# Loading and turning keys by pairs of heads, and VectorE alone for the first outer products, in a linear-attention and two-MoE kernel

## The chip, the core and the metric

One of the eight cores of a Trainium2 chip runs the program. Times are device microseconds (us) of one launch: the median of 3 runs of the kernel before is 305.4 (305.36, 305.4 and 305.83). Engines: PE is TensorE (PEld its weight loads), DVE VectorE, ACT ScalarE, POOL GpSimd, SP SyncE, which here only issues DMAs (SPq in the profile is its queue).

## The reference, cut to what matters

```python
def phi(x):                                   # x: batch 4, heads 4, seq 1088, dim 32; S1, S2: 8 x 32
    a = einsum('rd,bhsd->bhsr', S1, x)
    b = einsum('rd,bhsd->bhsr', S2, x)
    return outer product of a and b per token  # 64 features
q_p, k_p = phi(q), phi(k)
kv  = einsum('bhsf,bhsd->bhfd', k_p, v)
z   = sum of k_p over the sequence
x   = (q_p @ kv) / (q_p @ z + 1e-6)           # 4352 tokens x 128
xn  = x / rms(x) * rms_g                      # first MoE: 128 -> 1536 -> 128
x   = (silu(xn @ w_gate) * (xn @ w_val)) @ w_out
# second (soft) MoE: logits = x @ phi; softmax over tokens and over 32 slots; 8 experts of width 1024
```

S1, S2 and the weights of the first MoE come as 64-bit floats and are converted on the chip.

## The kernel before, in words

The 4352 tokens are nine tiles T: tiles 0 to 7 have 512 tokens each (tile T belongs to batch T // 2), tile 8 holds the last 64 tokens of every batch and head. For every tile the first MoE runs in twelve slots f of 128 hidden columns: `ff_in` makes the gate and value products g and v (lines 695 to 697, three matmuls each, since xh/xl and wgh/wgl are a high and a low part of the numbers), `ff_gate` the silu and the product hh or hf (lines 736, 737), `ff_out` the product with w_out. Queries of later tiles (`q_chain`) and keys of later batches (`k_chain`) are prepared between the slots.

Before the first slot stands the **front**: keys of batch 0 and queries of tile 0, since `ff_in` of tile 0 needs them. Its order is written by hand in the table `FRONT`, a list of tokens; every token is a step, and `in_order` keeps each engine's instructions in the order of the tokens. Outside of the front and its LOCK of 3 slots a scheduler of the build decides. The steps that matter here, with lines of the kernel before:

- `load_k`, `load_v`, `load_q`, `load_kr`: DMAs, all issued by SP in the order of the calls (line 79). `kt` is the key tile, `kr` the last 64 keys of every head, `vt` the values, `q0s` the first half of the queries of batch 0.
- `kt:c` (line 367) transposes a half of the keys on DVE into a tile T, `kt:2` the small keys (line 370), `qs` the queries (line 545).
- `b` and `bm` make the projection tables: bdk (line 304), for the keys, and bd (line 306), for queries and small keys.
- `kp` projects the keys on PE (line 388), `kg` the small keys (line 392), `qp` the queries (line 550).
- `kx:hp` (line 396) turns the projections of a pair hp of heads on DVE, `kh` (line 314) and `qh` (lines 314 and 557) copy them out of PSUM on ACT.
- `ko:g` and `qo:f` (line 319) are the outer products: `ko:0` and `ko:1` for the two pairs of heads, `ko:2` for the small keys, `qo:0` and `qo:1` for the queries. The letter behind is the engine (d is DVE, p is POOL, which can't read PSUM: `qh` therefore copies both halves for it).
- `kv:hp` copies V beside a column of ones (line 375, ACT, tile va).
- `ks:hp` sums over the tokens on PE (line 427: sixteen matmuls on the large keys, then two on the small ones), `kw` spreads the sums (line 442, ACT), `kb` transposes them (line 452, PE), `kl` places them as kvz (line 469: four copies for each pair).
- `qb` (line 565) turns the outer products of the queries, `qa` is the product with kvz (line 582), and `qd`, `qq`, `qr`, `qm`, `qt`, `qx`, `ql` are division, norm and the two parts xh and xl.
- `n:17` issues 17 matmuls on constants (line 333), whose results nobody reads. `c:g` is one step of converting weight group g: on ACT lines 217 and 270, on DVE lines 221 and 226, on POOL lines 233 and 278.

Wherever two steps name the same engine, the table decides which stands first; an engine that waits for an operand holds up all that stands behind it.

Of the kernel before, what the change touches and what calls it, by code (L numbers as in the profile page):

```python
# [8 lines left out]
F32 = mybir.dt.float32  # L9
# [7 lines left out]
P = 128  # L17
B, H, S, D, R = 4, 4, 1088, 32, 8
# [12 lines left out]
FRONT = """  # L31
n:17 b n:3 kz kt:0 bm kt:1 bm qs kp kt:2 kx:0 kx:1 ko:0:d ko:1:p:0 ko:1:d:1 qp kg kv:0 kv:1 qh kh ko:2:d qo:1:p n:4 km
ks:0 qo:0:d qb c:0 ks:1 kw:0:a kb:0 kw:1:a n:2 kb:1 n:10 c:0 c:0 kl:0:a kl:1:d c:0 c:1 c:0 c:1 c:0 c:0
qa n:34 qd:0 qd:1 qq:0:a qq:1:d qr:0 qq:2:a qq:3:d qr:1 c:1 kr:a qm:0 qm:1 qt:0 qx:0 n:2 qt:1 qx:1 c:1 c:1 ql c:2 c:2 c:2 c:1 c:2
# [16 lines left out]
def body(ctx, tc, q, k, v, s1, s2, wg, wv, wo, rg, phi, w1, w2, out):  # L51
# [24 lines left out]
    gate = [None]  # L76

    def load(out, in_, on=None):
        i = (on or nc.sync).dma_start(out=out, in_=in_)
        if gate[0] is not None:  # L80
            info = mybir.DependencyInfo(mybir.DependencyClass.Sync, mybir.DependencyReason.DATA)
            tc.add_manual_dep(i.ins, gate[0], info, reason="load in time")
# [13 lines left out]
    def load_k(b):  # L96

        t = ring()
        kt[b] = t.rearrange("p (h c m) -> p h c m", h=H, c=2)
        src = k[b, :, 0:1024, :].rearrange("h (c u e n) d -> c e u h (n d)", c=2, e=2, n=4)  # L100
        for c in range(2):
            for e in range(2):
                load(out=kt[b][64 * e : 64 * e + 64, :, c], in_=src[c, e])

# [4 lines left out]
    def load_v(b):  # L109

        t = ring()
        vt[b] = t.rearrange("p (h n d) -> p h n d", h=H, d=D)
        load(
            out=t.rearrange("p (h n) -> p h n", h=H),
            in_=v[b, :, 0:1024, :].rearrange("h (p j) d -> p h (j d)", j=8),
        )
        load(out=vr[:, :, 0:D], in_=v[b, :, 1024:, :].rearrange("h p d -> p h d"))
# [36 lines left out]
    load_k(0)  # L154
    rest_q = load_q(0)
    load_kr(0)
    load_v(0)
    load_w(w_keys[0])
    rest_q()
# [191 lines left out]
    class Keys:  # L351
# [12 lines left out]
        def transpose(self, c):  # L364
            if c < 2:
                self.kT[c] = row("T", 2)
                dve.transpose(self.kT[c].rearrange("p (h m) -> p h m", h=H), kt[self.b][:, :, c])
            else:
                self.kT[c] = sb.tile([P, 64], F32, tag="krT", name="krT")
                dve.transpose(self.kT[c].rearrange("p (x n) -> p n x", n=2), kr[self.b])  # L370
# [5 lines left out]

        def project(self, banks=1):
            for h in range(H):
                if h == 0 or h == 2 and banks == 2:
                    a = bank()  # L380
                self.a["k", h // 2] = a
                cs = slice(P * h, P * h + P)
                for c in range(2) if banks == 2 else (1, 0):
                    with ExitStack() as s:
                        s.enter_context(tc.issue_after(self.last) if self.last else nullcontext())
                        o = a[64 * c : 64 * c + 64, cs]
                        s.enter_context(tc.high_priority())
                        self.last = pe.matmul(o, bdk.rearrange("p h r -> p (h r)"), self.kT[c][:, cs], start=True, stop=True).ins

# [73 lines left out]

        def place_1(self, f, eng):
            av = self.a["T", 2 * f].rearrange("p (m e n) -> p m e n", e=2, n=64)[:, :, :, 0:D1]
            hv = self.kvz.rearrange("p f (a e) g c -> p (f a) e g c", e=2)
            for g in range(4):
                gs = slice(32 * g, 32 * g + 32)
                eng(hv[gs, 2 * f : 2 * f + 2, :, g % 2, :], av[gs, 2 * f : 2 * f + 2])
# [60 lines left out]
    class Queries:  # L530
# [21 lines left out]
        def halves(self):  # L552
            self.pq = work()[:, 0 : 256 * self.n].rearrange("p (f g n) -> p f g n", f=2, n=D)
            self.x1, self.x2 = proj_halves(self.a["q"], 4 * self.n, P)
            if self.T == 0:
                x2 = sb.tile([P, P], F32, tag="asb", name="asb", bufs=3).rearrange("p (g r) -> p g r", r=R)
                act.copy(x2, self.x2)
                self.x2 = x2

# [100 lines left out]
    def q_chain(T):  # L660
        q = Queries(T)

        with tc.issue_after(mark["gate", 1, 0] if T == 2 else mark["sq0"]) if T < 3 else nullcontext():
            q.shuffle()
# [244 lines left out]
    def spawn(c, phase, at=0):  # L909
        chains.append([c, phase, now + at])  # L910
# [45 lines left out]
    def front():  # L956
# [13 lines left out]
            "kt": lambda c: k.transpose(int(c)),  # L970
            "kp": lambda: k.project(2),
            "kg": k.project_r,
# [6 lines left out]
            "kb": lambda hp: k.back(range(2 * int(hp), 2 * int(hp) + 2), 2),  # L979
            "kl": lambda f, e: (k.place_1(int(f), copy[e]), kv_done.add(0)),  # L980
            "km": lambda: pool.memset(kvr.rearrange("p a h g c -> p (a h g c)"), 0.0),
# [34 lines left out]
    def start_tile(T):  # L1016
# [17 lines left out]
        if T < 2:  # L1034
            spawn(q_chain(T + 1), POST, 2 if T == 0 else 0)
        if T == 8:
# [303 lines left out]
```

## Time and profile before

| | us |
|---|---|
| median of 3 runs | 305.4 |
| the profiled execution, whole | 308.0 |
| its span | 306.2 |
| PE busy | 295.9 |
| DVE busy | 234.6 |
| ACT busy | 179.5 |
| POOL busy | 63.6 |

The profiled execution took 308.0 us, of which the span from the first to the last instruction is 306.2, so 1.8 lie around it. It is 2.6 longer than the median of the unprofiled runs. Starts are counted from the start of the span. A matmul on 32-bit data is shown as two records. Lengths of neighbouring instructions on one engine can overlap a little in the rows.

### The profile page before, as it was taken

The numbers are of one execution on the slowest core, as the hardware profiler recorded it, in microseconds if no ns is written. First come the engines' busy times: TensorE is split into PE (matmuls) and PEld (weight loads), VectorE is DVE, ScalarE is ACT, GpSimd is POOL, SyncE is SP. The second block draws the span as 40 slices with busy tenths as digits, with TensorE's granted clock in tenths as the row PEclk, the third lists the DMA queues.
The fourth block names the chain that finished last, engine by engine and source line by source line (L and its number), as shares of the span: only waits on it lengthen the run. The fifth ranks groups of instructions, "written<-read, shape, count | busy, mean of one in ns | idle before, by whom it ended". The sixth has DMA issues, their size and how long they took to land.

```text
span 306.2 us, 6349 instructions
## 1 busy us (share of the span) xinstructions
PE 295.9 (97%) x2372; PEld 233.6 (76%) x2372; DVE 234.6 (77%) x461; ACT 179.5 (59%) x400; POOL 63.6 (21%) x111
## 2 busy tenths in 40 slices
PE   6999989999999999999999999999999999999992
PEld 4887646687888888788887887888788788997481
DVE  3969975888699897988689888878796766675852
ACT  2378875356757456755654677466565756566461
POOL 2557899300601200110101001002001000003210
PEclk9599999999999999999999999999999999999999
DMA  5994300011016100010061000101936791000026
GB/s 146 310 370 122 108 0 1 2 16 20 0 43 183 26 6 0 4 25 10 23 200 27 2 3 6 25 5 19 346 60 177 192 321 42 0 0 3 2 75 220
DMA packets 40767, 24.04 MB, mean 78 GB/s; under 512 B 18080, under 2 KB 36768, under 8 KB 40736
## 3 DMA queue, kind: packets, MB, share of 16 engines
q1 hardware_dynamic: 40560, 23.56, 26.7%
q8 instruction: 19, 0.31, 0.4%
q10 hardware_dynamic: 176, 0.07, 0.1%
q14 instruction: 12, 0.10, 0.1%
HBM read 19.81 MB, written 2.23 MB: 72 GB/s over the span
## 4 chain that ended last, share of the span: by engine, by line
PE 84%; DVE 4%; POOL 4%; ACT 3%; DMA 1%; issue 1%; SPq 1%; DVEq 0%; ACTq 0%
PE o L697 7%; PE v L695 7%; PE g L695 7%; PE o L695 7%; PE v L697 7%; PE v L696 7%; PE g L696 7%; PE g L697 7%; PE o L696 7%; PE aux L427 2%; PE aux L582 2%; PE o L761 2%; PE aux L550 2%; POOL wgl L278 2%; PE fo L1291 2%; POOL hf L233 1%
## 5 line engine op out<-in xcount | busy, mean ns | idle before, releaser
L736 ACT ACTIVATE silu<-g 128x512 f32<-128x512 f32 (+1 forms) x103 | 60.8, 593 | 45.1 <-PE g L697 44.5
L746 ACT CAST hh<-hf 128x512 fp32r<-128x512 f32 x89 | 54.9, 617 | 33.4 <-DVE hf L737 32.6
L737 DVE TENSOR_TENSOR hf<-v,silu 128x512 f32<-128x512 f32 (+1 forms) x91 | 61.4, 676 | 16.1 <-ACT hh L746 7.1
L751 DVE TENSOR_TENSOR hl<-hf,hh 128x512 fp32r<-128x512 f32 x89 | 61.0, 688 | 15.2 <-ACT hh L746 14.1
L695 PE MATMUL g<-xh,wgh 128*128 128x512 f32 (+1 forms) x107 | 43.3, 404 | 0.8 <-ACT silu L736 0.8
L695 PE MATMUL v<-xh,wgh 128*128 128x512 f32 (+1 forms) x107 | 41.9, 391 | 0.4 <-DVE hh L737 0.4
L696 PE MATMUL g<-xh,wgl 128*128 128x512 f32 (+1 forms) x107 | 41.0, 383 | 0.0
L697 PE MATMUL v<-xl,wgh 128*128 128x512 f32 (+1 forms) x107 | 40.5, 379 | 0.0
L696 PE MATMUL v<-xh,wgl 128*128 128x512 f32 (+1 forms) x107 | 40.5, 378 | 0.0
L697 PE MATMUL g<-xl,wgh 128*128 128x512 f32 (+1 forms) x107 | 40.5, 378 | 0.0
L697 PE MATMUL o<-hl,woh 128*128 128x512 f32 (+1 forms) x94 | 37.2, 396 | 0.0
L695 PE MATMUL o<-hh,woh 128*128 128x512 f32 (+1 forms) x94 | 36.5, 389 | 0.0
L696 PE MATMUL o<-hh,wol 128*128 128x512 f32 (+1 forms) x94 | 35.6, 379 | 0.0
L631 POOL TENSOR_SCALAR rs<-ss 128x4 f32<-128x4 f32 (+1 forms) x8 | 1.9, 240 | 134.3 <-ACT sq L624 134.2
L695 PEld LDWEIGHTS g<-xh,wgh 128*128 128x128 f32 x107 | 20.1, 188 | 7.2 <-ACT silu L736 2.3
L696 PEld LDWEIGHTS g<-xh,wgl 128*128 128x128 f32 x107 | 20.1, 188 | 5.1 <-issue 0.7
L695 PEld LDWEIGHTS v<-xh,wgh 128*128 128x128 f32 x107 | 20.2, 189 | 4.8 <-DVE hh L737 1.0
L697 PEld LDWEIGHTS g<-xl,wgh 128*128 128x128 f32 x107 | 20.1, 188 | 4.0 <-issue 0.2
L697 PEld LDWEIGHTS v<-xl,wgh 128*128 128x128 f32 x107 | 20.1, 188 | 3.9
L696 PEld LDWEIGHTS v<-xh,wgl 128*128 128x128 f32 x107 | 20.1, 188 | 3.7 <-issue 0.2
L695 PEld LDWEIGHTS o<-hh,woh 128*128 128x128 f32 x94 | 17.7, 188 | 4.0 <-issue 0.8
L697 PEld LDWEIGHTS o<-hl,woh 128*128 128x128 f32 x94 | 17.7, 188 | 3.7 <-issue 0.2
(278 smaller groups left out, 491.4 us busy)
## 6 DMA issues: line engine op xcount, KB each, us to landing
ring<-in_moe_w_dram SPq DMA_DIRECT2D x12, 256.0 KB, 7.0
ring<-in_moe_w_dram SPq DMA_DIRECT2D x5, 512.0 KB, 4.4
ring<-in_k_dram SPq DMA_DIRECT2D x16, 128.0 KB, 2.9
ring<-in_v_dram SPq DMA_DIRECT2D x4, 512.0 KB, 5.6
ring<-in_moe_w_gate_dram SPq DMA_DIRECT2D x6, 256.0 KB, 5.6
ring<-in_moe_w_val_dram SPq DMA_DIRECT2D x6, 256.0 KB, 6.6
ring<-in_moe_w_out_dram SPq DMA_DIRECT2D x3, 512.0 KB, 7.8
qt<-in_q_dram SPq DMA_DIRECT2D x3, 512.0 KB
```

The source lines that it names most:

```text
L278: i = pool.tensor_tensor(out=dl[:, ts], in0=src[:, ts], in1=dh[:, ts].bitcast(F32), op=ALU.subtract)
L427: pe.matmul(self.a["kv", hp][64 * h2 : 64 * h2 + self.cols, 64 * hp : 64 * hp + 64], (va_all if t < 8 else vr_all)[:, v0 : v0 + self.cols] ...
L550: pe.matmul(self.a["q"][:, 64 * h : 64 * h + 64], self.qD[:, P * h : P * h + P], bdf, start=True, stop=True)
L582: last = pe.matmul(o, pD[rs, f, h, cs], rhs, start=(f == 0), stop=(f == 1)).ins
L695: first = pe.matmul(o, ah, bh, start=start, stop=False)
L696: pe.matmul(o, al, bh, start=False, stop=False)
L697: last = pe.matmul(o, ah, bl, start=False, stop=stop)
L736: mark["silu"] = act.activation(s[:, cs], g[:, cs], AF.Silu).ins
L737: mark["gate"] = mark["gate", T, f] = dve.tensor_tensor(out=hf32[T, f][:, cs], in0=v[:, cs], in1=s[:, cs], op=ALU.mult).ins
L746: act.copy(hh[T, f], hf32[T, f])
L751: dve.tensor_tensor(out=hl[T, f], in0=hf32.pop((T, f)), in1=hh[T, f].bitcast(F32), op=ALU.subtract)
L761: last = pe.matmul(ops[T][:, 0:w], w_c, h[:, cs], start=(c == 0), stop=(c == NF - 1))
```

## The change

Keys of a batch come in two DMAs of 128 partitions (a pair of heads each, pieces of 1 KB) where there were four of 64 partitions (pieces of 512 bytes); V comes in four of 64 partitions where there was one of 128. `kt:c` and `kp:hp` work on a pair of heads, and `kp` is two steps. In the order of SP's DMAs for batch 0, `kr`, V and the small V go before the queries. (`kr` was issued by SyncE before too.) All five outer products of the front are DVE's, `qh` copies one half only, and `kl:1` is split between ACT and DVE. `qs` moves behind `ko:0`, `qp` behind `ks:0`, and `n:4` becomes `n:8` in another place. In the main part, the queries of tile 1 start one slot later and are tied to another product of line 737.

```diff
@@ -29,8 +29,8 @@
 
 
 FRONT = """
-n:17 b n:3 kz kt:0 bm kt:1 bm qs kp kt:2 kx:0 kx:1 ko:0:d ko:1:p:0 ko:1:d:1 qp kg kv:0 kv:1 qh kh ko:2:d qo:1:p n:4 km
-ks:0 qo:0:d qb c:0 ks:1 kw:0:a kb:0 kw:1:a n:2 kb:1 n:10 c:0 c:0 kl:0:a kl:1:d c:0 c:1 c:0 c:1 c:0 c:0
+n:17 b n:3 kz kt:0 bm kt:1 bm kp:0 kp:1 kx:0 kx:1 kt:2 ko:0:d kg kv:0 kv:1 kh qs ko:1:d n:8 ko:2:d km
+ks:0 qp qh qo:0:d qo:1:d qb c:0 kw:0:a ks:1 kb:0 kw:1:a n:2 kb:1 n:10 c:0 kl:0:a kl:1:a:0:2 kl:1:d:2:4 c:0 c:0 c:0 c:1 c:0 c:1 c:0 c:0
 qa n:34 qd:0 qd:1 qq:0:a qq:1:d qr:0 qq:2:a qq:3:d qr:1 c:1 kr:a qm:0 qm:1 qt:0 qx:0 n:2 qt:1 qx:1 c:1 c:1 ql c:2 c:2 c:2 c:1 c:2
 """
 
@@ -97,10 +97,10 @@
 
         t = ring()
         kt[b] = t.rearrange("p (h c m) -> p h c m", h=H, c=2)
-        src = k[b, :, 0:1024, :].rearrange("h (c u e n) d -> c e u h (n d)", c=2, e=2, n=4)
-        for c in range(2):
-            for e in range(2):
-                load(out=kt[b][64 * e : 64 * e + 64, :, c], in_=src[c, e])
+        src = k[b, :, 0:1024, :].rearrange("h (p j) d -> p h (j d)", j=8)
+        for hp in range(2):
+            hs = slice(2 * hp, 2 * hp + 2)
+            load(out=t.rearrange("p (h m) -> p h m", h=H)[:, hs], in_=src[:, hs])
 
     def load_kr(b):
         kr[b] = sb.tile([P, 2 * D], F32, tag="kr", name="kr")
@@ -110,10 +110,10 @@
 
         t = ring()
         vt[b] = t.rearrange("p (h n d) -> p h n d", h=H, d=D)
-        load(
-            out=t.rearrange("p (h n) -> p h n", h=H),
-            in_=v[b, :, 0:1024, :].rearrange("h (p j) d -> p h (j d)", j=8),
-        )
+        src = v[b, :, 0:1024, :].rearrange("h (e u c n) d -> c e u h (n d)", e=2, c=2, n=4)
+        for c in range(2):
+            for e in range(2):
+                load(out=t.rearrange("p (h e m) -> p e h m", h=H, e=2)[64 * c : 64 * c + 64, e], in_=src[c, e])
         load(out=vr[:, :, 0:D], in_=v[b, :, 1024:, :].rearrange("h p d -> p h d"))
 
     def load_q(b):
@@ -152,9 +152,9 @@
     w_keys = [("gv", 0), ("gv", 1), ("o", 0), ("gv", 2), ("gv", 3), ("o", 1), ("gv", 4), ("gv", 5), ("o", 2)]
     load_s()
     load_k(0)
-    rest_q = load_q(0)
     load_kr(0)
     load_v(0)
+    rest_q = load_q(0)
     load_w(w_keys[0])
     rest_q()
     load_w(w_keys[1])
@@ -364,7 +364,7 @@
         def transpose(self, c):
             if c < 2:
                 self.kT[c] = row("T", 2)
-                dve.transpose(self.kT[c].rearrange("p (h m) -> p h m", h=H), kt[self.b][:, :, c])
+                dve.transpose(self.kT[c], kt[self.b][:, 2 * c : 2 * c + 2].rearrange("p h c m -> p (h c m)"))
             else:
                 self.kT[c] = sb.tile([P, 64], F32, tag="krT", name="krT")
                 dve.transpose(self.kT[c].rearrange("p (x n) -> p n x", n=2), kr[self.b])
@@ -374,18 +374,17 @@
             src = vt[self.b][:, hs].rearrange("p h t d -> p (h t) d")
             eng(va[:, hs, :, 0:D].rearrange("p h t d -> p (h t) d"), src)
 
-        def project(self, banks=1):
-            for h in range(H):
+        def project(self, hps=range(2), banks=1):
+            for h in range(2 * hps.start, 2 * hps.stop):
                 if h == 0 or h == 2 and banks == 2:
-                    a = bank()
-                self.a["k", h // 2] = a
-                cs = slice(P * h, P * h + P)
-                for c in range(2) if banks == 2 else (1, 0):
-                    with ExitStack() as s:
-                        s.enter_context(tc.issue_after(self.last) if self.last else nullcontext())
-                        o = a[64 * c : 64 * c + 64, cs]
-                        s.enter_context(tc.high_priority())
-                        self.last = pe.matmul(o, bdk.rearrange("p h r -> p (h r)"), self.kT[c][:, cs], start=True, stop=True).ins
+                    self.a["k"] = bank()
+                a = self.a["k", h // 2] = self.a["k"]
+                for c in range(2):
+                    with tc.high_priority(), tc.issue_after(self.last) if self.last else nullcontext():
+                        o = a[64 * c : 64 * c + 64, P * h : P * h + P]
+                        m = P * (2 * (h % 2) + c)
+                        rhs = self.kT[h // 2][:, m : m + P]
+                        self.last = pe.matmul(o, bdk.rearrange("p h r -> p (h r)"), rhs, start=True, stop=True).ins
 
         def project_r(self):
             self.a["r"] = bank()
@@ -461,10 +460,10 @@
                 act.copy(hv[gs, :, :, g % 2, :], av[gs])
             self.place_r(slice(0, 2))
 
-        def place_1(self, f, eng):
+        def place_1(self, f, eng, g0=0, g1=4):
             av = self.a["T", 2 * f].rearrange("p (m e n) -> p m e n", e=2, n=64)[:, :, :, 0:D1]
             hv = self.kvz.rearrange("p f (a e) g c -> p (f a) e g c", e=2)
-            for g in range(4):
+            for g in range(g0, g1):
                 gs = slice(32 * g, 32 * g + 32)
                 eng(hv[gs, 2 * f : 2 * f + 2, :, g % 2, :], av[gs, 2 * f : 2 * f + 2])
 
@@ -552,10 +551,6 @@
         def halves(self):
             self.pq = work()[:, 0 : 256 * self.n].rearrange("p (f g n) -> p f g n", f=2, n=D)
             self.x1, self.x2 = proj_halves(self.a["q"], 4 * self.n, P)
-            if self.T == 0:
-                x2 = sb.tile([P, P], F32, tag="asb", name="asb", bufs=3).rearrange("p (g r) -> p g r", r=R)
-                act.copy(x2, self.x2)
-                self.x2 = x2
 
         def outer(self, f, on=dve):
             outer(self.pq[:, f], self.x1[:, :, 4 * f : 4 * f + 4], self.x2, on)
@@ -660,7 +655,7 @@
     def q_chain(T):
         q = Queries(T)
 
-        with tc.issue_after(mark["gate", 1, 0] if T == 2 else mark["sq0"]) if T < 3 else nullcontext():
+        with tc.issue_after(mark["gate", T - 1, 0 if T == 2 else 1]) if T < 3 else nullcontext():
             q.shuffle()
         yield PE, 0
         q.project()
@@ -968,7 +963,7 @@
             "bm": lambda: next(placed, None),
             "kz": k.zero,
             "kt": lambda c: k.transpose(int(c)),
-            "kp": lambda: k.project(2),
+            "kp": lambda hp: k.project(range(int(hp), int(hp) + 1), 2),
             "kg": k.project_r,
             "kx": lambda hp: k.turn(slice(int(hp), int(hp) + 1), turned),
             "kh": k.halves_r,
@@ -977,7 +972,7 @@
             "ks": lambda hp: k.sum(int(hp), range(9), 2),
             "kw": lambda hp, e: k.spread_1(int(hp), copy[e]),
             "kb": lambda hp: k.back(range(2 * int(hp), 2 * int(hp) + 2), 2),
-            "kl": lambda f, e: (k.place_1(int(f), copy[e]), kv_done.add(0)),
+            "kl": lambda f, e, *g: (k.place_1(int(f), copy[e], *map(int, g)), kv_done.add(0)),
             "km": lambda: pool.memset(kvr.rearrange("p a h g c -> p (a h g c)"), 0.0),
             "kr": lambda e: k.place_r(slice(0, 2), copy[e]),
             "qs": q.shuffle,
@@ -1032,7 +1027,7 @@
             load_v(b)
             spawn(k_chain(b), PE, 8 if b == 1 else 0)
         if T < 2:
-            spawn(q_chain(T + 1), POST, 2 if T == 0 else 0)
+            spawn(q_chain(T + 1), POST, 3 if T == 0 else 0)
         if T == 8:
             w = work()[:, 0 : 2 * DM].rearrange("p (c n) -> p c n", n=DM)
             h, l = (t[:, NF - 2 :, :].bitcast(F32) for t in (woh, wol))
```

On DVE, the front between the table bdk and the turning of the queries' outer products (T holds transposed keys, silu the turned projections, work the outer products, pkr those of the small keys). Before:

```order
L367 STREAM_TRANSPOSE T<-ring 128x512
L306 TENSOR_TENSOR bd<-aux,blk 128x64
L545 STREAM_TRANSPOSE x_196<-x 128x512
L370 STREAM_TRANSPOSE krT<-kr 128x2x32
L396 STREAM_TRANSPOSE silu<-aux 128x256
L396 STREAM_TRANSPOSE silu<-g 128x256
L319 TENSOR_TENSOR work<-silu 128x1024
L319 TENSOR_TENSOR work<-silu 128x512
L319 TENSOR_TENSOR pkr<-asb,aux 64x256
L319 TENSOR_TENSOR work<-asb 128x512
L565 STREAM_TRANSPOSE work<-work 128x1024
```

The same stretch of DVE in the changed kernel:

```order
L367 STREAM_TRANSPOSE T<-ring 128x512
L306 TENSOR_TENSOR bd<-aux,blk 128x64
L395 STREAM_TRANSPOSE silu<-aux 128x256
L395 STREAM_TRANSPOSE silu<-g 128x256
L370 STREAM_TRANSPOSE krT<-kr 128x2x32
L319 TENSOR_TENSOR work<-silu 128x1024
L544 STREAM_TRANSPOSE x_218<-x 128x512
L319 TENSOR_TENSOR work<-silu 128x1024
L319 TENSOR_TENSOR pkr<-asb,v 64x256
L319 TENSOR_TENSOR work<-asb,g 128x512 x2
L560 STREAM_TRANSPOSE work<-work 128x1024
```

The transpose of the queries went from ahead of the first outer product to behind it, the second outer product is whole, and both of the queries' stand here.

On PE, the front from the projections of the keys on, before (v<-bd,x is the projection of the queries):

```order
L388 MATMUL aux<-T,bdk 64x128 x4
L388 MATMUL g<-T,bdk 64x128 x4
L550 MATMUL v<-bd,x_196 128x64 x4
L392 MATMUL aux<-bd,krT 64x64
L333 LDWEIGHTS hot
L333 MATMUL idle<-hot 128x256
```

In the changed kernel, the sums over the tokens on PE (aux<-work,va and v<-work,va), with the projection of the queries, g<-bd,x:

```order
L426 MATMUL aux<-work,va 64x64 x16
L426 MATMUL aux<-pkr,vr 64x64 x2
L549 MATMUL g<-bd,x_218 128x64 x4
L426 MATMUL v<-work,va 64x64 x16
L426 MATMUL v<-pkr,vr 64x64 x2
```

The projection of the queries went from ahead of all sums to between those of the two pairs of heads.

On DVE in the slots of tile 0, around the outer products of the queries of tile 1 (work<-asb,aux; cvs and ring belong to the conversion of weights, hh to the slots), before:

```order
L226 SCALAR_TENSOR_TENSOR cvs<-ring,hf 128x512
L737 TENSOR_TENSOR hh<-v,silu 128x512
L319 TENSOR_TENSOR work<-asb,aux 128x512 x2
L221 TENSOR_SCALAR ring<-ring 128x512
L565 STREAM_TRANSPOSE work<-work 128x1024
L737 TENSOR_TENSOR hh<-v,silu 128x512
L226 SCALAR_TENSOR_TENSOR cvs<-ring 128x512
```

and in the changed kernel:

```order
L226 SCALAR_TENSOR_TENSOR cvs<-ring,hf 128x512
L732 TENSOR_TENSOR hh<-v,silu 128x512 x2
L221 TENSOR_SCALAR ring<-ring 128x512
L226 SCALAR_TENSOR_TENSOR cvs<-ring 128x512
L319 TENSOR_TENSOR work<-asb,aux 128x512 x2
L221 TENSOR_SCALAR cvt<-cvt 128x512
L560 STREAM_TRANSPOSE work<-work 128x1024
```

The step cvs<-ring of the weights stands ahead of the outer products where it stood behind them and their transpose.

## Rows read from the trace of the kernel before

**Rows 1.** Page, part 1: busy us, share of the span, instructions of each engine.
```profile
PE 295.9 (97%) x2372; PEld 233.6 (76%) x2372; DVE 234.6 (77%) x461; ACT 179.5 (59%) x400; POOL 63.6 (21%) x111
```

**Rows 2.** Chain of waits, first 24 us: start, length, what.
```profile
2.87 3.65 DMA ring<-in_k_dram
...
8.86 1.90 PE v L550 x8
...
12.13 2.32 PE g L427 x36
14.45 1.50 PE v L427 x36
```

**Rows 3.** Windows: busy PE, PEld, DVE, ACT, POOL (instructions), granted clock, DMA share, GB/s.
```profile
7.90:8.40 0.50, 0.50 (x9) 0.50 (x5) 0.50 (x3) 0.00 (x0) 0.00 (x0) 0.53 0.93 272
...
14.90:15.40 0.50, 0.50 (x25) 0.50 (x21) 0.16 (x1) 0.00 (x0) 0.00 (x0) 1.00 1.07 399
```

**Rows 4.** Timeline of DVE: start, length, instruction [idle before it, releaser].
```profile
4.86 0.71 DVE L367 STREAM_TRANSPOSE T<-ring 128x512 f32<-128x512 f32 x1
5.49 0.19 DVE L304 TENSOR_TENSOR bdk<-aux,blk 128x64 f32<-128x64 f32 x1
...
8.89 0.45 DVE L396 STREAM_TRANSPOSE silu<-g 128x256 f32<-128x256 f32 x1 [0.38 <-PE g L388]
9.27 2.66 DVE L319 TENSOR_TENSOR work<-silu 128x1024 f32<-128x1024 f32 x2
...
13.51 1.25 DVE L565 STREAM_TRANSPOSE work<-work 128x1024 f32<-128x1024 f32 x1
14.68 0.39 DVE L221 TENSOR_SCALAR cvt<-cvt 128x512 uint32<-128x512 uint32 x1
...
16.84 1.20 DVE L469 COPY kvz<-aux 32x132 f32<-32x132 f32 x4 [1.78 <-PE aux L452]
```

**Rows 5.** Groups of DVE by shape, whole span: busy us, mean ns | idle before.
```profile
L319 DVE TENSOR_TENSOR work<-asb,aux 128x512 f32<-128x512 f32 x14 | 8.9, 681 | 1.2 <-ACT asb L314 1.1
L319 DVE TENSOR_TENSOR work<-x 128x1024 f32<-128x1024 f32 x6 | 7.0, 1212 | 0.0
L319 DVE TENSOR_TENSOR pkr<-asb,aux 64x256 f32<-64x256 f32 x4 | 1.6, 407 | 0.8 <-ACT asb L314 0.8
L319 DVE TENSOR_TENSOR work<-silu 128x512 f32<-128x512 f32 x1 | 1.6, 1557 | 0.0
```

**Rows 6.** Timeline of PE: start, length of the records together.
```profile
7.38 0.54 PE L388 MATMUL aux<-T,bdk 128*64 128x128 f32 x5 [1.21 <-DVE T L367]
...
19.08 3.88 PE L333 MATMUL idle<-hot 128*128 128x256 bf16 x34
...
28.20 1.00 PE L550 MATMUL aux<-bd,T 128*128 128x64 f32 x8
```

**Rows 7.** Timeline of ACT.
```profile
9.67 1.14 ACT L375 COPY va<-ring 128x512 f32<-128x512 f32 x2 [5.51 <-DMA ring<-in_v_dram]
...
16.83 1.06 ACT L469 COPY kvz<-aux 32x132 f32<-32x132 f32 x4
```

**Rows 8.** Timeline of SP's queue: start and length of the issues.
```profile
0.73 2.75 SPq L79 DMA_DIRECT2D ring<-in_k_dram  x4
...
4.89 0.43 SPq L79 DMA_DIRECT2D ring<-in_v_dram  x1
```

**Rows 9.** DMA issues, first 10 us: count, KB each, median us from issue to landing.
```profile
ring<-in_k_dram SPq DMA_DIRECT2D x4, 128.0 KB, 3.2
...
x<-in_q_dram SPq DMA_DIRECT2D x1, 256.0 KB, 3.6
qt<-in_q_dram SPq DMA_DIRECT2D x1, 256.0 KB, 5.1
```

**Rows 10.** Timeline of POOL in the slots of tile 0.
```profile
36.50 2.04 POOL L233 TENSOR_TENSOR ring<-cvs,cvc 128x256 uint32<-128x256 uint32 x2 [1.18 <-DVE cvs L226]
```

**Rows 11.** Waits of PE from 24.2 us on: us in total, times, longest.
```profile
PE g L695 <- ACT silu L736: 0.8, 2, 0.4
```

## The prediction

> **What bounds the kernel now.** I read the busy shares first: PE is busy for 295.9 of 306.2 us [rows 1], so what can be gained lies where PE waits or works slowly. The list of PE's waits from 24.2 us on names one of 0.8 us in two pieces as its longest entry [rows 11]: behind the front there is little to win. So the front is next, and its view is the chain of waits in order of time [rows 2]. It goes from the last of four key DMAs (landed at 6.52) over PE's projection of the queries (1.90 us), the sums of the first pair (2.32) and those of the second pair (1.50). The two groups of sums are the same 36 records, so the first ran slower; the windows show why: the granted clock is 0.53 in 7.9 to 8.4 and 1.00 from 14.9 on [rows 3], half of 2.4 GHz and then all of it. Before it fell, PE had done one projection of keys and then waited 1.21 us for the second transposed half T [rows 6]. In between, PE itself is the chain: it works without a gap at the lower level while DVE's results wait for it.
>
> The end of the front is the product of the queries with kvz, which needs the placing copies: ACT and DVE make four each, 1.06 us and 1.20 us, and DVE's end at 16.84 + 1.20 = 18.04 [rows 4, 7]. I follow the change up to the last of these copies; all behind it up to the first slot is the same list of steps.
>
> **The change, step by step.**
>
> *Keys.* SP issued four key DMAs in 2.75 us, 0.69 each, and the last landed at 6.52 [rows 2, 8]. With two, the second is issued at 0.73 + 0.69 = 1.42. Landing 3.2 us later [rows 9], or 3.65 as the last one of before [rows 2], gives 4.6 to 5.1; it is twice as big, but even one more 0.69 gives 5.8. DVE can't start the second transpose before the table bdk is done at 5.49 + 0.19 = 5.68 [rows 4], so the DMA is hidden or nearly so. The transpose takes 0.71 [rows 4], to 6.4. PE projects the first pair from 5.7: five records took 0.54 [rows 6], 0.108 each, so the eight of a pair take 0.87, to 6.6, and the second pair follows without a gap, to 7.4. Before, the second turning started at 8.89 and the first outer product at 9.27 [rows 4], 0.38 later; now the turning can start at 7.45, and with some 0.2 for the small keys' transpose, which now stands behind it (my estimate: an eighth of the elements of a 0.71 transpose and a start), the outer product starts at 8.1 where it started at 9.27.
>
> *Outer products.* One of 1024 elements takes 1.21 alone, and one of 512 from PSUM 0.68, but the half beside POOL's took 1.56 [rows 5]. So `ko:0` ends at 9.3. `ko:1` was 1.56 on DVE and is now 1.21; POOL's two are gone. On DVE the queries' second product adds 0.68.
>
> *Queries.* Their DMA is now the ninth issue: 0.73 + 8 x 0.69 = 6.2, landing 3.6 later [rows 9] at 9.8. DVE, done with `ko:0` at 9.3, waits 0.5 for it. This is the wait that the change adds, and `ko:1`, `ko:2` and all the rest of DVE's list stand behind it. `qs` is a transpose of 0.71, to 10.5; `ko:1` to 11.7; `ko:2` (0.41 [rows 5]) to 12.1.
>
> *V.* The fourth piece is issued at 0.73 + 6 x 0.69 = 4.9, as the single one was [rows 8]. It lands at 8.1 by the 3.2 of key pieces of this size [rows 9], at 9.7 if it needs the time of before, when ACT's copies started at 9.67 [rows 7]. With 1.14 for the copies, the sums can start at 9.3 to 10.8. Sixteen matmuls are 32 of 36 records, 1.33 us of 1.50, so they end at 10.6 to 12.1 and both ends are covered by `ko:2` at 12.1. The Trainium skill (DMA: Bandwidth & Descriptors, section Rules for kernel authors) advises against splitting a transfer into partition halves, since the halves share the same DMA engines; that speaks against the four pieces. By it V would be no earlier than 9.7, and the sum would be the same by that cover.
>
> *PE from there.* Two matmuls on the small keys end the first sums at 12.3. The queries' projection, now behind them, takes 1.00 at the full clock [rows 6], to 13.3. A copy of one half on ACT, about as long as a placing copy (1.06 / 4), and the hand-over make it 13.6. DVE then does two outer products (1.36), the turning (1.25) and a step of the weights (0.39) [rows 4, 5]: 15.0, 16.2, 16.6; then its two placing copies, 0.30 each, to 17.2. PE meanwhile does the second sums, 1.50, from 13.3 to 14.8. From the end of these sums to the first placing copy it took 16.83 - 15.95 = 0.88 [rows 2, 7], so ACT starts at 15.7 and makes six at 0.265: 17.3. The last copy thus ends at 17.3 where it ended at 18.04: the front gains 0.7. Bounds: if the queries are there at 9.3, 1.2 is gained; if they take the 5.1 of their other half [rows 9], they land at 11.3, 1.5 later than I assume, and 0.8 is lost.
>
> *The eight idle matmuls* took 3.88 / 34 = 0.11 each [rows 6], 0.9 in all, and lie in PE's wait for `ko:0` (small keys at 8.3, first sums at 9.3): nothing. At the half clock they are 1.8 and end at 10.1, still under the 12.1.
>
> *Slots of tile 0.* POOL adds the weight words there, and once stood idle for 1.18 us because DVE's cvs came late [rows 10]; ahead of it on DVE were the outer products and the turning of tile 1's queries. Now that cvs stands ahead of them. PE would get at most the 0.8 that it waited for silu, which stands behind casts on ACT that wait for POOL [rows 11]. The same move puts tile 1's queries one slot later, into a fuller stretch near its own first slot: no row shows that; I bound the loss by 0.5, a little over the longest single wait of PE there, 0.4 [rows 11]. Between -0.8 and +0.5 I take -0.4, half of what PE waited.
>
> *Nothing*: that SyncE issues the small keys is no change of engine, only of place. In later batches there are three more V issues and two fewer for keys, one more by 0.69, on a queue that nobody behind the front is seen to wait for on PE.
>
> Sum: -0.7 - 0.4 = -1.1. The profiled execution took 308.0 (span 306.2 and 1.8 around it), so it would take 306.9. The median of the unprofiled runs is 2.6 lower; I carry the difference over: 305.4 - 1.1 = **304.3 us**.
>
> **The rivals.**
>
> *The clock falls again, and the gain turns into a loss.* Between the keys' projection and the sums PE has only the small keys and 0.9 us of idle matmuls, and it waits from about 10.6 to 12.1 for `ko:2`. If the granted clock is half from then on, the sums of the first pair are covered, but the queries' projection takes 1.90 for 1.00 and the second sums 2.32 for 1.50 [rows 2, 6], 1.7 more in a row on the path. The front loses 1.0 instead of gaining 0.7: with -0.4 behind it, +0.6, 306.0. It decides if the fall comes before 12.3. For it: a wait of 1.21 was followed by a fall. Against it: the sixteen records of projections now stand close together where one projection and a hole stood. The Trainium skill (TensorE: Matmul & The Clock Gate, part 1, The HAM clock gate) states that half rate is the state of an idle engine and work lifts it; the rows agree in direction.
>
> *The queries land late.* Eight issues now lie ahead of them, V among them. At 11.3, as bounded above, the sum is +0.4: 305.8. From 10.5 on the front gains nothing. For it: V took 9.67 - 4.89 = 4.8 to land [rows 7, 8] and now goes ahead of the queries. Against it: the keys are through the queue earlier.
>
> *Tile 0 takes it back.* If the move of tile 1's queries costs 0.5 instead of giving 0.4, the sum is -0.2: 305.2, within what can be told from no change.
>
> **How the numbers follow.** I give my forecast 0.52, the clock 0.17, the late queries 0.16, tile 0 0.15. A measurement of this kernel tells about 0.2%, 0.6 us, from no change. The forecast, from -2.0 to -0.3 by its bounds, is faster in 0.45 and the same in 0.07; the clock is slower in 0.12 and the same in 0.05 (if it comes back before the second sums); the late queries are slower in 0.07, the same in 0.06, faster in 0.03; tile 0 is the same in 0.07, faster in 0.05, slower in 0.03. Sums: faster 0.53, same 0.25, slower 0.22. The range is 303.1 to 306.2: the forecast's better end (305.4 - 2.0 = 303.4) and a little, and the clock's price with a little. The forecast's own range is 303.4 to 305.1.
>
> **What would show it.** In the profile after: both halves T transposed by 6.5 and no wait of PE between the projections; the first outer product at about 8.1; a wait of DVE for the DMA of the queries of about 0.5; a granted clock of 1.00 from 8 to 15; the last placing copy at about 17.3; the first matmul of the slots (line 720) 0.7 earlier than before; POOL's wait of 1.18 gone. The forecast is wrong if the clock is half under the queries' projection, if DVE waits over 1.2 for the queries, or if tile 1's first slot waits for xh or xl.

## The result: slower by 1.0%, against a forecast of faster

The kernel after takes 308.56 us (308.11 to 309.4, 4 runs), the kernel before 305.48 beside it: the ratio is 1.0102, 95% interval 1.0079 to 1.0126. I had forecast 304.3, with 306.2 as the upper end.

In the profile after, the whole execution takes 308.61 and its span 306.8. PE's busy time is 1.1 below that of [rows 1], and yet the span is 0.6 longer than the 306.2 of before:

```profile
span 306.8 us, 6365 instructions
...
PE 294.8 (96%) x2376; PEld 231.6 (75%) x2376; DVE 234.0 (76%) x460; ACT 179.5 (58%) x401; POOL 61.1 (20%) x109
```

The front first. This is DVE's timeline (start, length, instruction, idle time before it and its releaser), to be held against [rows 4]:

```profile
4.66 0.69 DVE L367 STREAM_TRANSPOSE T<-ring 128x512 f32<-128x512 f32 x1
...
5.54 0.70 DVE L367 STREAM_TRANSPOSE T<-ring 128x512 f32<-128x512 f32 x1
...
7.84 1.18 DVE L319 TENSOR_TENSOR work<-silu 128x1024 f32<-128x1024 f32 x1
9.23 0.71 DVE L544 STREAM_TRANSPOSE x<-x 128x512 f32<-128x512 f32 x1 [0.21 <-DMA x<-in_q_dram]
9.87 1.18 DVE L319 TENSOR_TENSOR work<-silu 128x1024 f32<-128x1024 f32 x1
10.97 0.40 DVE L319 TENSOR_TENSOR pkr<-asb,v 64x256 f32<-64x256 f32 x1
13.13 1.28 DVE L319 TENSOR_TENSOR work<-asb,g 128x512 f32<-128x512 f32 x2 [1.76 <-ACT asb L314]
...
16.76 0.61 DVE L468 COPY kvz<-aux 32x132 f32<-32x132 f32 x2 [0.76 <-issue]
```

The first outer product starts at 7.84 (9.27 before), DVE waits 0.21 for the queries, and then 1.76 for `qh`. The reason for the 1.76 is in PE's timeline, to be held against [rows 6]: the queries' projection (line 549) stands behind the two small-key matmuls, and these wait 1.07 for `ko:2`.

```profile
5.94 0.91 PE L387 MATMUL aux<-T,bdk 128*64 128x128 f32 x8
6.68 0.61 PE L387 MATMUL g<-T,bdk 128*64 128x128 f32 x8
...
9.21 1.15 PE L426 MATMUL aux<-work,va 128*64 128x64 f32 x32
11.43 0.33 PE L426 MATMUL aux<-pkr,vr 64*64 64x64 f32 x4 [1.07 <-DVE pkr L319]
11.69 1.10 PE L549 MATMUL g<-bd,x 128*128 128x64 f32 x8
12.73 1.15 PE L426 MATMUL v<-work,va 128*64 128x64 f32 x32
...
17.42 0.28 PE L577 MATMUL g<-kvz,work 64*64 64x66 f32 x2 [0.86 <-DVE kvz L468]
...
23.54 0.39 PE L715 MATMUL g<-xh,wgh 128*128 128x256 f32 x1
```

The clock did not fall. The windows of [rows 3], now (the eighth column is the granted clock):

```profile
7.90:8.40 0.50, 0.43 (x4) 0.35 (x5) 0.50 (x2) 0.50 (x2) 0.00 (x0) 1.00 1.06 313
14.90:15.40 0.50, 0.50 (x7) 0.45 (x5) 0.50 (x1) 0.35 (x2) 0.00 (x0) 1.00 1.08 416
```

ACT's rows, beside [rows 7]: V is copied from 7.62 on (9.67 before), and the six placing copies end at 16.68. DVE's two follow 0.08 later, though DVE was idle for 0.76: the split of `kl:1` by groups of 32 partitions, two for each engine, did not make them run side by side.

```profile
7.62 1.14 ACT L375 COPY va<-ring 128x512 f32<-128x512 f32 x2 [3.51 <-DMA ring<-in_v_dram]
...
15.04 1.64 ACT L468 COPY kvz<-aux 32x132 f32<-32x132 f32 x6 [0.45 <-PE aux L451]
```

So the first slot starts at 23.54, and in the profiled execution of before it started at 24.22: 0.68 earlier, as forecast. The loss must lie behind it, or in what the 24.22 stands for. Behind it, PE's list of waits has one entry that differs from [rows 11]:

```profile
PE g L690 <- ACT silu L731: 0.8, 1, 0.8
```

The total is the same 0.8, but it is one piece where before had two of 0.4, and it stands at the start of tile 1. PE's timeline there:

```profile
58.02 0.39 PE L690 MATMUL g<-xh,wgh 128*128 128x512 f32 x1
...
59.02 1.09 PE L426 MATMUL aux<-work,va 128*33 128x64 f32 x32
...
60.39 1.09 PE L426 MATMUL aux<-work,va 128*33 128x64 f32 x32
61.41 0.50 PE L692 MATMUL g<-xl,wgh 128*128 128x512 f32 x1
...
62.21 0.39 PE L692 MATMUL v<-xl,wgh 128*128 128x512 f32 x1
63.43 0.50 PE L690 MATMUL g<-xh,wgh 128*128 128x512 f32 x1 [0.83 <-ACT silu L731]
```

and ACT's in the same stretch:

```profile
61.58 1.17 ACT L437 COPY kvT<-aux 33x512 f32<-33x512 f32 x2 [2.13 <-PE aux L426]
62.78 1.09 ACT L731 ACTIVATE silu<-g 128x512 f32<-128x512 f32 x2
```

Two slots of tile 1 are begun with xh alone; then come 2.4 us of sums over the keys of batch 1, and only then the products with xl that finish the two slots. ACT has nothing to do for 2.13 us, then two copies of those sums, and only then the silu that PE waits for. From the start of the last product with xl, 62.21, to the start of the next matmul, 63.43, are 1.22 us, where 61.75, 61.98 and 62.21 follow each other at 0.23: PE loses about 1.0 at this point. POOL's wait of 1.18 [rows 10] became 0.69.

### The profile page after: what moved, and what is told of

Same layout as the page of the kernel before. It is cut to its first block, busy times and chain, and to the rows that moved or that the text cites. A ratio compares the mean times of both kernels' runs of the same rounds, so it can differ in the third digit from the quotient of the medians.

```text
span 306.8 us, 6365 instructions
## 1 busy us (share of the span) xinstructions
PE 294.8 (96%) x2376; PEld 231.6 (75%) x2376; DVE 234.0 (76%) x460; ACT 179.5 (58%) x401; POOL 61.1 (20%) x109
## 4 chain that ended last, share of the span: by engine, by line
PE 83%; DVE 4%; ACT 1%; issue 0%; DVEq 0%
PE v L690 8%; PE g L690 7%; PE v L691 7%; PE o L690 7%; PE v L692 7%; PE o L692 7%; PE g L691 7%; PE g L692 7%; PE o L691 7%; PE o L756 3%; PE aux L577 3%; PE aux L426 2%; PE aux L549 2%; PE fo L1286 2%; PE aux L638 1%; PE aux L773 1%
```

## The experiments

Medians are against the kernel before on the same chip. "First slot" is the start of the first matmul of the slots in the run's profile (line 720 in before's numbering, 715 in after's; where a run adds lines, the numbers shift by a few).

### Before once more, and the move of tile 1's queries taken apart

The first run is the kernel before, unchanged.

> The kernel before, unchanged, profiled once more. Theory A: the profiled execution of before was not like the timed ones: its clock was half from 7.9 to 14.8 us, and the 2.6 us between it (308.0) and the median (305.4) are that stretch. Then a new profiled execution near 305.5 has a span near 303.6, the granted clock at 1.00 between 5 and 15 us, the first slot's matmul near 21.6 us instead of 24.2, and the rest of the program as long as before. Rival B: the stretch at half clock is in every execution of before, and the 2.6 us are the profiler's; then the clock is half again, the first slot is at 24.2 and the span is 306.2.

Measured: 305.42 us, and a profiled execution of 305.01 (span 303.2), where the one on which I predicted took 308.0. PE's timeline of this one, against [rows 6]:

```profile
6.55 0.54 PE L388 MATMUL aux<-T,bdk 128*64 128x128 f32 x5 [0.17 <-DVE T L367]
...
7.56 1.10 PE L550 MATMUL v<-bd,x 128*128 128x64 f32 x8
...
10.10 1.15 PE L427 MATMUL g<-work,va 128*64 128x64 f32 x32 [0.63 <-ACT va L375]
...
21.54 0.39 PE L720 MATMUL g<-xh,wgh 128*128 128x256 f32 x1
```

The wait for T is 0.17 and not 1.21, the queries' projection takes 1.10, the granted clock reads 1.00 up to there, and the first slot starts at 21.54. This is what most executions look like: they take the same time, and the mean granted clock on record is 0.993 to 0.999 in 89 of 92 executions of the kernel before, beside 0.987 in the one on which I predicted. That one was a rare one, in which the key landed late and the clock fell: its front was 24.22 - 21.54 = 2.7 longer. Measured against 21.54, the front after is 2.0 longer, not 0.7 shorter.

The second run is the kernel after with the old start and the old tie of tile 1's queries; the third is the kernel before with the new ones.

```diff
-with tc.issue_after(mark["gate", T - 1, 0 if T == 2 else 1]) if T < 3 ...
+with tc.issue_after(mark["gate", 1, 0] if T == 2 else mark["sq0"]) if T < 3 ...
-spawn(q_chain(T + 1), POST, 3 if T == 0 else 0)
+spawn(q_chain(T + 1), POST, 2 if T == 0 else 0)
```

> The changed kernel, with the queries of tile 1 started as in before (one slot earlier, tied to the square of tile 0). Theory A: the changed start costs 1.2 us, most of it PE's wait of 0.83 for silu at the start of tile 1; without it the time is 307.3 (308.5 - 1.2), the wait at 63 us is gone, and what is left against before (+1.9) is the front. Rival B (the front gains 0.7 in timed runs too, and the main part loses all of the 3.1 and the 0.7): 304.7.

> The kernel before, with the queries of tile 1 started as in the changed kernel. Theory A: +1.2, 306.7, with a wait of PE for silu at the start of tile 1 and the front as in before. Rival B: +3.8, 309.3. Rival C (the later start only hurts together with the changed front): 305.5.

Measured: 307.29 (ratio 1.0047, 1.0024 to 1.007) and 306.80 (1.0044, 1.0026 to 1.0062). From both sides the move costs 1.3 us: 308.56 - 307.29, and 306.80 - 305.48. In the second run PE's wait of 0.83 is gone (two of 0.4 stand in its list, as in [rows 11]), and the products with xl that finish the first two slots stand ahead of the sums over the keys of batch 1:

```profile
58.51 0.39 PE L692 MATMUL v<-xl,wgh 128*128 128x512 f32 x1
...
60.38 1.09 PE L426 MATMUL aux<-work,va 128*33 128x64 f32 x32
```

In the third the wait is there, in a kernel that has nothing else of the change:

```profile
63.83 0.50 PE L695 MATMUL g<-xh,wgh 128*128 128x512 f32 x1 [0.82 <-ACT silu L736]
```

The move is two edits. The next two runs take back one each in the kernel after: the slot (3 to 2), or the tie.

> The kernel after, with the start of tile 1's queries one slot earlier again, as in the kernel before, but still tied to the later product of line 737. Which of the two edits holds the 1.27 us that e2 gave back? If it is the slot at which the chain starts: 307.3 us, and the wait of 0.83 of PE for silu at tile 1's first slot is gone. If it is the tie: 308.5, and the wait stands.

> The kernel after, with the old tie of tile 1's queries, but still started one slot later. By the theory that the slot of the start sets it: 308.5 us, with the wait of 0.8 of PE. By the theory of the tie: 307.3 and no such wait.

Measured: 307.1 (1.0046, 1.003 to 1.0063) and 310.1 (1.0157, 1.0133 to 1.018). The start sets it: with the start one slot earlier the tie makes no difference that can be told (307.1 and 307.29; PE's list has no wait for silu in the first). With the late start the new tie helps, and without it another 1.5 us is lost, which neither theory had. In that run the first slot starts at 24.10 and not at 23.54, and PE waits for silu twice, 1.8 in all, and longer for the products (0.9 against 0.7 in the kernel after):

```profile
PE g L690 <- ACT silu L731: 1.8, 2, 1.0
...
PE v L690 <- DVE hh L732: 0.9, 2, 0.8
```

### Is it the hole that brings the clock down?

The hole is PE's wait for the second T, 1.21 in [rows 6]. The kernel before with its hole filled, by `n:12` in place of `n:3`:

> The kernel before with twelve idle matmuls instead of three ahead of the projection of the keys, so that PE has work while it waits for the second half of the keys. Theory A: the timed executions of before run the front at the full clock anyway, so the time stays (305.5 within 0.6) and the profile shows 1.00 from 5 to 15 us with the first slot near 21.6. Rival B (the clock is half there in every execution of before): 2.6 are gained, 302.9.

Measured: 305.58 (1.0003, 0.9987 to 1.002), first slot 21.98, 0.4 later than in the unchanged run: the twelve matmuls end at 7.46, behind the 6.55 at which PE goes on there. Where the clock does not fall, filling is worth nothing. So the next pair makes the hole, in the kernel before: the last key DMA is issued behind the queries' first one, and then the same with `n:15`.

```diff
-    load_k(0)
+    last_k = load_k(0)          # issues three of its four DMAs
     rest_q = load_q(0)
+    last_k()
```

> The kernel before, with the last of the four key DMAs issued behind the queries' first one. Its issue moves by about 0.7 us, so the second half T comes about 0.7 later, and PE's wait between the two projections grows from 0.17 (e1) to about 0.9, near the 1.21 of the profiled execution of before. Theory: that hole brings the clock down in all executions; then the first pair's projections, the queries' projection and the first sums run at half speed, and it takes about 305.5 + 2.7 = 308.2 us. Rival: the hole alone doesn't, and the later key costs at most its own 0.7: 305.5 to 306.2, first slot at 21.5 to 22.3.

> As the run before, with twelve idle matmuls more (0.11 each, 1.3 us) ahead of the projections, so that PE works through the hole. If the hole brings the clock down and costs 2.7: filled, it takes 306.2 or less. If the clock doesn't hang on this hole: the same time as without the filling, within 0.3.

Measured: 308.39 (1.0089, 1.0055 to 1.0122) and, filled, 306.13 (1.0016, 0.9999 to 1.0034). PE's timeline of the first of the two:

```profile
7.81 0.90 PE L392 MATMUL aux<-T,bdk 128*64 128x128 f32 x5 [1.95 <-DVE T L371]
...
9.71 1.97 PE L554 MATMUL v<-bd,x 128*128 128x64 f32 x8
```

and of the filled one, where the key came no earlier (DVE's second transpose starts at 7.48, against 7.04 without the filling):

```profile
5.19 2.15 PE L337 MATMUL idle<-hot 128*128 128x256 bf16 x15
...
8.25 0.54 PE L392 MATMUL aux<-T,bdk 128*64 128x128 f32 x5 [0.54 <-DVE T L371]
...
9.27 1.10 PE L554 MATMUL v<-bd,x 128*128 128x64 f32 x8
```

Their windows from 8 to 13 us, in the same order:

```profile
8.00:13.00 5.00, 5.00 (x30) 3.90 (x28) 4.24 (x7) 2.29 (x6) 2.65 (x2) 0.50 1.06 298
```

```profile
8.00:13.00 5.00, 4.21 (x64) 3.52 (x64) 5.00 (x10) 2.25 (x6) 3.09 (x2) 1.00 1.02 312
```

After the wait of 1.95 the clock is half (1.2 of 2.4 GHz) from 8 to 13 us, though PE is busy for all of it. With the wait down to 0.54 it is full, and matmuls that nobody reads take 2.3 us off the time. The mean granted clock of the executions goes the same way: with the hole 0.985 to 0.987 in four of six, filled 0.994 to 0.998 in all twelve. That is the theory, with one limit: of the other two executions with the hole one took 305.91 at 0.999 (and one 309.68 at 0.994), so the fall does not come every time. The pair also parts the late key from the fall: filled, the late key alone costs 306.13 - 305.44 = 0.7, hardly clear of noise, and the fall 2.3 more.

### The front of the kernel after

Three steps, each on top of the one before, all with the old start of tile 1's queries. First the queries' projection is moved into PE's wait for `ko:2` (`sum` gets a range):

```diff
-ks:0 qp qh qo:0:d ...
+ks:0:0:8 qp ks:0:8:9 qh qo:0:d ...
```

> The changed kernel with the old start of tile 1's queries (its time is 307.3) and, in the front, the projection of the queries moved on PE from behind the first pair's sums into the wait before their two last matmuls. Theory A (the front lost against a full-clock front because 1.04 us of that projection stand ahead of the second pair's sums): the second sums begin 1.0 earlier, the first slot starts at 22.4 instead of 23.4, the time is 306.3. Rival D (the front lost because VectorE alone is late with the outer products): the products end at the same time as now, so nothing moves, 307.3.

Measured: 306.2 (1.0025, 1.0015 to 1.0035), first slot 22.46; 1.1 us less than the 307.29 without it. DVE's wait for `qh` shrinks from 1.76 to 0.66:

```profile
11.79 1.28 DVE L319 TENSOR_TENSOR work<-asb,g 128x512 f32<-128x512 f32 x2 [0.66 <-ACT asb L314]
...
15.68 0.61 DVE L468 COPY kvz<-aux 32x132 f32<-32x132 f32 x2 [1.02 <-issue]
```

Next, the placing copies as before, four for each engine:

```diff
-kl:0:a kl:1:a:0:2 kl:1:d:2:4
+kl:0:a kl:1:d
```

> As the run before, and the placing copies split as before the change: four on ACT, four on DVE. Theory A (with three quarters on ACT, DVE's two copies start only when ACT's six are done, at 16.76, after DVE stood idle 0.76): DVE's four run beside ACT's again, the last ends 0.4 earlier than in the run before, 305.9. Rival E (DVE waits for the same thing whatever the split): 306.3 or more.

Measured: 305.55 (1.0007, 0.9999 to 1.0016), another 0.65 less, first slot 22.07. DVE's four copies now start at 14.71, beside ACT's:

```profile
14.71 1.19 DVE L468 COPY kvz<-aux 32x132 f32<-32x132 f32 x4
```

At this point the change costs nothing that can be told. What is left of it is the loads by pairs and VectorE alone. Can these gain, if the queries also keep their early place? The third step issues the queries right behind the keys and puts `qs` and `qp` where the kernel before has them:

```diff
+    rest_q = load_q(0)
     load_kr(0)
     load_v(0)
-    rest_q = load_q(0)
-... bm kp:0 kp:1 kx:0 kx:1 kt:2 ko:0:d kg kv:0 kv:1 kh qs ko:1:d n:8 ko:2:d km
-ks:0:0:8 qp ks:0:8:9 qh qo:0:d ...
+... bm qs kp:0 kp:1 kx:0 kx:1 kt:2 ko:0:d ko:1:d qp kg kv:0 kv:1 qh kh ko:2:d n:4 km
+ks:0 qo:0:d ...
```

> The changed kernel's loads of keys by pairs, V in four pieces and outer products on VectorE alone, but the queries loaded behind the keys, turned and projected ahead of the sums as in before, the placing copies as in before, and tile 1's queries started as in before. Theory A: the first outer product starts near 7.9, the last key product ends near 10.7, the first slot starts near 20.9, and the time is 304.8, 0.6 under the kernel before (305.4). Rival F: V, now behind the queries, holds the sums up, and the time is that of before, 305.4. Rival D (VectorE alone is too slow): 306 or more.

Measured: 305.01 beside 305.38 for before (0.9995, 0.998 to 1.0009): not told apart, and between theory A and rival F. Its first slot starts at 21.21, 0.33 ahead of the 21.54. The last run gives a half of the second outer product and one of the queries' back to POOL:

```diff
-ko:0:d ko:1:d qp ... n:4 km        -ks:0 qo:0:d qo:1:d qb
+ko:0:d ko:1:p:0 ko:1:d:1 qp ... qo:1:p n:4 km        +ks:0 qo:0:d qb
```

> As the run before, with a half of the second outer product and one of the queries' on GpSimd, as in the kernel before. Theory A (beside GpSimd the half on VectorE takes 1.56 for 0.6, so GpSimd gives nothing): 0.3 slower than the run before, 305.1. Rival D (two engines are faster than one): 0.4 faster, 304.4.

Measured: 305.14 (0.9993, 0.9984 to 1.0001), first slot 21.55. The keys' products on DVE, first with VectorE alone, then beside POOL:

```profile
7.98 2.32 DVE L319 TENSOR_TENSOR work<-silu 128x1024 f32<-128x1024 f32 x2
```

```profile
7.91 2.66 DVE L319 TENSOR_TENSOR work<-silu 128x1024 f32<-128x1024 f32 x2
```

Both rows show the shape of their first product alone: the first one is two products of 1024 elements, the second one of 1024 and a half one. So with POOL at work DVE takes 0.34 longer for three quarters of the elements, and in the whole time the two are the same. No version beat the kernel before by what can be measured.

## Why the prediction was wrong

Its steps in the front came out, one by one: the first outer product at 7.84 (forecast 8.1), a wait for the queries of 0.21 (0.5), V covered, the clock at 1.00, the idle matmuls free, the last placing copy at 17.37 (17.3), the first slot 0.68 earlier than in the profile (0.7). The last two agree by luck. PE was through the second sums at 14.14, where I had 14.8, and DVE was free for its copies at 16.00, where I had 16.6; the 0.6 in hand went into the 0.76 for which DVE then stood idle, a wait that I did not have. Two other steps failed.

*"The median of the unprofiled runs is 2.6 lower; I carry the difference over."* This one turned the sign. The 2.6 was no constant offset of profiling: it was a key that landed late and the clock's fall behind it, and it lay in the very stretch that I costed. All that the front could win by keeping the clock up was won against an execution that the other runs are not like. The rows on record were enough to suspect it: the queries' projection took 1.90 and 1.00 elsewhere [rows 2, 6], the first sums 2.32 and the second 1.50 [rows 2]. That is 1.7 of the 2.6 in two rows, and I had written both down as a price. With 305.4 as an execution at full clock, the same working gives a front that is 2.7 - 0.7 = 2.0 longer.

*Slots of tile 0, taken as -0.4.* The move of tile 1's queries costs 1.3. I had bounded the loss at 0.5 by the longest wait of PE there, but a wait that exists does not bound one that a new order makes. My list of signs against the forecast had the right place, tile 1's first slot waiting for xl, only that PE does not stand still for it: it runs 2.4 us of sums in between, and ACT comes late. The gain that I set against it did not come: POOL's wait is 0.69 with the new tie and 1.18 with the old one, both with the old start, and the times are 307.1 and 307.29.

The two corrections make 305.4 + 2.0 + 1.3 = 308.7, and 308.56 was measured; both corrections are taken from the runs, so this closes the sum and tests nothing. By the runs, the 3.1 us are about 1.3 for the move of tile 1's queries, 1.0 to 1.1 for `qp` behind the first sums, 0.65 for the split of the placing copies, and 0.2 that is not told from nothing.

Within the front, then, it is the hand-written order that loses, and I had not priced it: I put `qp` at 12.3 and called all ahead of it covered, without asking when the kernel before has the projection done at full clock (8.7 in the unchanged run). I had also let DVE's two placing copies follow DVE's own list; by the rows they start 0.08 after the end of ACT's six, and 0.09 after it in the run with `qp` in the wait.

Of the rivals, the clock falling again and the late queries did not happen. The third, tile 0 taking it back, had the direction and less than half the size.

V was there earlier than the 9.7 that I had as its earliest by the Trainium skill (DMA: Bandwidth & Descriptors, section Rules for kernel authors), which advises against partition halves: ACT's copies start at 7.62. This is no clean test, since the queries no longer go ahead of V. In the run with the queries ahead of V again the copies start at 8.28, against 9.43 in the unchanged run, but there V's first piece is issued at 3.09 and not at 4.89.

On the clock, the Trainium skill (TensorE: Matmul & The Clock Gate, part 1, The HAM clock gate) states that half rate is the state of an idle engine, and work lifts it. The pair with the late key agrees in direction, half after a wait of 1.95 and full with the wait filled; but it also shows 0.50 from 8 to 13 us with PE busy throughout, so work did not lift it at once.

What stays open: why T landed late in that one profiled execution (the key's DMA landed at 6.52 [rows 2]); and why DVE's placing copies start behind ACT's. The run shows only that the split is what costs. In the kernel the two shares of `kl:1` read one PSUM tile, `kl:0` and `kl:1` two different ones; that this is the reason is not shown.

## What to carry to other kernels

Before costing a stretch, hold the profiled execution's own time against the median: a gap of 2.6 us was time that only this execution spent, and where the slow rows lie in the stretch that a change removes, the gain is not there in the other runs. A table of steps is to be costed by what stands behind the moved step on its engine, at the clock of the other runs: here one projection behind a wait cost 1.1, and putting it into that wait gave it back. A chain that starts one slot later can break up the next tile's work, which no wait of the old profile bounds.

## What was not expected of the hardware

The same late key was followed by half the clock in some executions and not in others: five took 308.3 to 309.7 and one 305.91. And the granted-clock column can miss half speed. In the profile of the kernel before with the new start of tile 1's queries, PE waits only 0.22 for T, and its rows are as long as at half speed:

```profile
5.19 0.82 PE L333 MATMUL idle<-hot 128*128 128x256 bf16 x3
...
6.85 0.90 PE L388 MATMUL aux<-T,bdk 128*64 128x128 f32 x5 [0.22 <-DVE T L367]
...
8.75 1.97 PE L550 MATMUL v<-bd,x 128*128 128x64 f32 x8
...
12.02 1.98 PE L427 MATMUL g<-work,va 128*64 128x64 f32 x32
...
14.20 1.15 PE L427 MATMUL v<-work,va 128*64 128x64 f32 x32
```

while the window says 1.00:

```profile
7.90:8.40 0.50, 0.50 (x8) 0.50 (x4) 0.40 (x1) 0.00 (x0) 0.00 (x0) 1.00 1.17 332
```

The wait did not slow them, for the three idle matmuls ahead of it are long already. In the profiled execution on which I predicted they took 0.50, and there the clock fell later:

```profile
5.10 0.50 PE L333 MATMUL idle<-hot 128*128 128x256 bf16 x3
```

The trace's list of clock changes explains the column. Its first entry, a rise to full, stands at 13.98 us in this run, between the long sums and the short ones; it stands at 5.87 in the unchanged run, at 6.51 in the kernel after and at 4.52 in the execution on which I predicted. Ahead of the first entry the column reads 1.00 in all of them, while the rows there are long: 0.80 and 0.82 for the three idle matmuls in the unchanged run and the kernel after. So the column is no evidence ahead of that entry, and the length of a row whose shape is known elsewhere is the safer sign. Why the rise came so late in this one execution was not settled. A late rise would also leave the mean clock high, as in five of the 92 executions of the kernel before, which took 307.2 to 307.6 at a mean of 0.997 or 0.998; that it was one there is not shown.
